# FFN matmuls that read their moving columns alternately from the two halves of a tile

## The chip, the cores and the metric

The kernel runs on one core of a Trainium2 chip. Its time is the device time of one execution in microseconds (us); the number compared is the median of several runs.

## The reference

The program computes a linear-attention layer with a decaying state (4 batches, 8 heads, 768 steps, 48 columns a head) and feeds its output to a two-layer network with a sigmoid GELU. The second part takes most of the time:

```python
def _moe_ref(x, w_in, w_out):        # x: 3072 x 384, w_in: 384 x 2048, w_out: 2048 x 384
    h = x @ w_in
    g = h * (1.0 / (1.0 + np.exp(-1.702 * h)))
    return (g @ w_out).astype(np.float32)
```

## The kernel before

Work is held transposed: features lie on the 128 partitions and tokens along the free dimension. The 3072 tokens are cut into 24 chunks of 128, and six groups of four chunks (512 tokens, `WIDE`) go through the FFN. Each group has 16 tasks, one for every 128 of the 2048 hidden features, 96 tasks in all.

The FFN is held to fp32 accuracy by splitting. Every operand is a pair of FP32R tensors, a rounded high part and the small rest, and each product is three matmuls: high by high, high by low, low by high. A task of the first product is 3 feature blocks by 3 terms, so 9 matmuls of 512 moving columns into one PSUM bank `ph`; a task of the second product is again 9, three for each of the banks `po0` to `po2`, which add up over the 16 tasks of a group. The moving operand of the first product is `xs[i][:, part, c, cs]`, a contiguous run of 512 4-byte words on each partition; that of the second is `gh` or `gl`, also 512 contiguous words.

Between the two products `gelu` runs: ScalarE writes `gh` (line 395) and `gf` (line 396) from the bank `ph`, and VectorE their difference `gl` (line 397).

The first 32 tasks, and the last one, use the whole 128-row array: `first_product` (lines 384 to 386) and `second_product` (lines 410 to 412). Tasks 32 to 94 are split into two halves of 64 rows (`first_rows`, `second_rows`, all through line 436 in `on_rows`). The two halves of the array run at the same time, one matmul of 64 rows in each; which of them stand side by side is written out in `rows_of`. A half of a matmul with 64 rows also has 512 columns.

The attention chunks (`chunk`) are put between the FFN tasks by an order written by hand: the string `RAMP` up to task 31, the list `PARTS` after it. It has its own small matmuls (lines 264 to 354), VectorE scans, and ScalarE work. `keep_clock` (line 425) are filler matmuls of 512 bf16 columns of zeros that stand in the first 46 us, before the FFN has data.

When a group is done, `store` copies each `po` bank to SBUF with one ScalarE instruction (line 511), 512 columns in order, and starts its DMA to the output. For the last group the third copy comes after the last matmul.

TensorE takes its instructions in the order of the program. Each matmul has its own load of 128 weight columns (PEld in the profile), which runs while the matmul ahead of it is streaming.

Of the kernel before, what the change touches and what calls it, by code (L numbers as in the profile page):

```python
# [13 lines left out]
AF = mybir.ActivationFunctionType  # L14
# [12 lines left out]
C = P  # L27
# [3 lines left out]
NF = DFF // P  # L31
NM = DM // P
# [8 lines left out]
W_SCALE = 2.0 ** 8  # L41
# [41 lines left out]
def rwkv_ffn_kernel(ctx: ExitStack, tc, wkr, vp, vrk, ub, w_in, w_out, masks, vt, uc, out):  # L83
    nc = tc.nc
    V, A, G, T = nc.vector, nc.scalar, nc.gpsimd, nc.tensor
# [27 lines left out]
        out=after, in_=after, pattern=[[1, C]], base=0, channel_multiplier=-1,  # L113
# [85 lines left out]
    def weight(which, f, m):  # L199

        s, n = divmod(f * NM + m, WP // P)
        return (pairs[2 * s + which][:, t, n * P : (n + 1) * P] for t in range(2))
# [172 lines left out]

    xs, po, parts, measures, tiled, steady = {}, {}, {}, {}, [], []

    def first_product(j, task):
        i, c0, c1, f = task
        cs = slice(c0 * C, c1 * C)  # L380
        ph = ps_h.tile([P, WIDE], F32, tag="ph", name="ph")[:, 0 : (c1 - c0) * C]
        for c in range(NM):
            h_, l_ = weight(0, f, c)
            T.matmul(ph, h_, xs[i][:, 0, c, cs], start=c == 0, stop=False)  # L384
            T.matmul(ph, h_, xs[i][:, 1, c, cs], start=False, stop=False)  # L385
            T.matmul(ph, l_, xs[i][:, 0, c, cs], start=False, stop=c == NM - 1)  # L386
        parts[j] = ph

    def gelu(j, task):
# [10 lines left out]
    def second_product(j, task):  # L400
        i, c0, c1, f = task
        gh, gl = parts.pop(j)
        first = i not in po
        if first:
            po[i] = [ps_o.tile([P, WIDE], F32, tag=f"po{m}", name=f"po{m}") for m in range(NM)]
        for m in range(NM):
            h_, l_ = weight(1, f, m)
            o = po[i][m][:, c0 * C : c1 * C]

            T.matmul(o, h_, gh, start=first, stop=False, skip_group_check=True)  # L410
            T.matmul(o, l_, gh, start=False, stop=False, skip_group_check=True)  # L411
            T.matmul(o, h_, gl, start=False, stop=f == NF - 1, skip_group_check=True)  # L412

    idle = []

# [17 lines left out]
    def on_rows(half, bank, out, w, x, start, stop, done):  # L433

        rows = slice(half * HB, (half + 1) * HB)
        mm = T.matmul(out, w[rows], x[rows], start=start, stop=stop, skip_group_check=True)  # L436
        before = relay.pop(bank, None)
        if before:
            tc.add_manual_dep(mm.ins, before, SYNC, reason="the bank's other row tile is done")
        if done:  # L440
            nop = nc.sync.nop()  # L441
            tc.add_manual_dep(nop.ins, mm.ins.name, SYNC, reason="a row tile is done with a bank")
            relay[bank] = nop.ins.name

    def first_rows(j, half):

        i, c0, c1, f = TASKS[j]
        cs = slice(c0 * C, c1 * C)
        if half == 0:
            parts[j] = ph_tile(c1 - c0)  # L450
        for n in range(3 * NM):
            c, term = divmod(n, 3)
            h_, l_ = weight(0, f, c)
            w, x = ((h_, 0), (h_, 1), (l_, 0))[term]
            end = n == 3 * NM - 1
            on_rows(
                half, ("h", j), parts[j], w, xs[i][:, x, c, cs],
                half == 0 and n == 0, half == 1 and end, half == 0 and end,
            )
            yield  # L460

    def second_rows(j, half):

        i, c0, c1, f = TASKS[j]
        gh, gl = parts[j]
        for n in range(3 * NM):
            m, term = divmod(n, 3)
            m = (m + half) % NM
            h_, l_ = weight(1, f, m)
            w, g = ((h_, gh), (l_, gh), (h_, gl))[term]  # L470
            tiles = po.setdefault(i, [None] * NM)
            start = tiles[m] is None
            if start:
                tiles[m] = ps_o.tile([P, WIDE], F32, tag=f"po{m}", name=f"po{m}")
            on_rows(
                half, ("o", i, m), tiles[m][:, c0 * C : c1 * C], w, g,
                start, f == NF - 1, term == 2,
            )
            yield
# [25 lines left out]
    def store(i, start, N, order=range(NM)):  # L505

        for m in order:
            o = po[i][m]
            ob = pools["late"].tile([P, WIDE], F32, tag="ob", name="ob", bufs=3)[:, 0:N]
            late = m != order[0] and isinstance(start, int) and start + N == NTOK  # L510
            A.activation(ob, o[:, 0:N], AF.Copy, scale=1.0 / W_SCALE)
            (A if late else queue[0]).dma_start(out[m, :, bass.ds(start, N)], ob)
        po.pop(i)
        xs.pop(i)
# [5 lines left out]
    with tc.manual_schedule():  # L520
# [17 lines left out]
        def do(token):  # L538
            kind, i = token[0], int(token[1:] or 0)
            told[token] = told.get(token, 0) + 1  # L540
            if kind in "lamwrf":
                piece(kind, i)
                if kind == "w" and all(told.get(f"w{n}") == 4 for n in range(2 * NL)):
                    early.close()
                    pools["late"] = fast.enter_context(tc.tile_pool(name="late", bufs=2))
            elif kind == "x":
                group, col = where[i]
                if col == CHUNKS[group] - 1:
                    fill_x(xs[group], 0, (col + 1) * C)
            elif kind == "u":  # L550
                nc.sync.dma_start(u_sb, ub)
            elif kind == "M":
                A.dma_start(hm[TOP:R2], masks)
                for x in states + [v[:, 0:TOP] for v in values]:
                    G.memset(x, 0.0)
            elif kind == "k":
                for _ in range(i):
                    keep_clock()
            elif kind == "g":
                first_product(i, TASKS[i])  # L560
            elif kind == "h":
                gelu(i, TASKS[i])
            elif kind == "y":
                second_product(i, TASKS[i])
            if kind == "y" or kind == "r" and told[token] == 2:
                i -= LAG if kind == "r" else 0
                parts.pop(i, None)
                group = TASKS[i][0]
                if i == last[group]:
                    store(group, starts[group] * C, CHUNKS[group] * C, (1, 0, 2) if kind == "r" else range(NM))  # L570
# [58 lines left out]
    with tc.If(n < full):  # L629
# [5 lines left out]
        with tc.tile_pool(name="gp", bufs=1) as gp, tc.tile_pool(name="ob", bufs=2) as ob, tc.For_i(0, B, 1) as b:  # L635
            pools["late"] = ob
            xg = [new_x(i) for i in range(2)]
            for p in range(NP):
# [7 lines left out]
                for d in range(D):  # L646
                    rows = []
                    for i, c0 in enumerate((1 + p * CW, 1 + NP * CW + p * C, 1 + NP * CW + NP * C + p * C)):
                        x = gp.tile([R2, CB, C], F32, tag=f"row{i}", name=f"row{i}", bufs=2)
# [16 lines left out]
                for half in range(2):  # L666
                    x = xg[half]
# [3 lines left out]
            for half in range(2):  # L671
                xs[half] = xg[half]
                for f in range(NF):
                    task = half, 0, 3, f
                    first_product(f, task)
                    gelu(f, task)
                    second_product(f, task)
                store(half, b * S + half * 384, 384)
# [54 lines left out]
```

## Time and profile before

| | us |
|---|---|
| median of 3 runs | 528.33 |
| the runs | 527.12, 528.33, 528.34 |
| span of the profiled execution, first to last instruction | 526.4 |
| TensorE matmul busy | 514.5 (98%) |
| TensorE weight loads busy | 437.0 (83%) |
| VectorE busy | 295.8 (56%) |
| ScalarE busy | 284.5 (54%) |

The profiled execution is known by its span; the median of the runs is 1.9 us longer, which is what lies ahead of the first and behind the last instruction. A matmul's record covers its way through the array, so records of matmuls that follow one another overlap: what one costs in a dense stretch is the step from start to start, not its duration.

### The profile page before, as it was taken

To read this page: it belongs to the slowest core of one execution; us is meant where nothing else is said; L and a number is where in the kernel's file an instruction comes from. 1 tells how busy PE (TensorE), PEld (TensorE's weight loads), DVE (VectorE), ACT (ScalarE), POOL (GpSimd) and SP (SyncE) were. 2 spreads that over 40 slices of the span, in tenths; PEclk is the share of its full clock that TensorE was granted. 3 is DMA by queue.
4 is the path that set the end of the run, shared out by engine and by line. 5 is a ranking of instruction groups with operands and counts; after the bars stand their busy time and mean duration, and the time that the engine had idled before them with its cause. 6 is when DMAs were issued, how large, how long until landed. Compare 5 with 4: busy or idle time off the path is not lost.

```text
span 526.4 us, 11132 instructions
## 1 busy us (share of the span) xinstructions
PE 514.5 (98%) x4539; PEld 437.0 (83%) x4539; DVE 295.8 (56%) x447; ACT 284.5 (54%) x609; POOL 42.6 (8%) x93
## 2 busy tenths in 40 slices
PE   7999999999999999999999999999999999999995
PEld 3766888888888888899999899999988998888873
DVE  7899999999884215656455455555555322111110
ACT  3988989877754714635445546545545422323222
POOL 2002000002000200201003021003020002100000
PEclk9999999999999999999999999999999999999999
DMA  8997921045633300152104062204050001100001
GB/s 291 289 393 215 346 93 61 2 164 140 220 110 107 76 0 1 45 183 86 67 2 136 2 226 61 91 2 137 2 159 1 1 1 31 61 2 1 0 1 66
DMA packets 14938, 50.95 MB, mean 97 GB/s; under 512 B 2336, under 2 KB 4384, under 8 KB 14880
## 3 DMA queue, kind: packets, MB, share of 16 engines
q1 hardware_dynamic: 9792, 31.83, 17.8%
q0 software_dynamic: 4688, 17.82, 11.0%
q8 instruction: 37, 0.61, 0.5%
q10 hardware_dynamic: 400, 0.53, 0.3%
q14 instruction: 21, 0.17, 0.1%
HBM read 43.09 MB, written 4.72 MB: 91 GB/s over the span
## 4 chain that ended last, share of the span: by engine, by line
PE 89%; DVE 2%; ACT 1%; DMA 1%; POOL 1%; issue 0%; ACTq 0%; SPq 0%
PE po L436 26%; PE ph L436 24%; PE ph L384 5%; PE po L410 4%; PE ph L385 4%; PE ph L386 4%; PE po L411 4%; PE po L412 4%; PE ps_y L346 4%; PE ps_s L331 4%; PE ps_y L354 3%; PE ps_u L312 1%; DMA x<-x 1%; POOL x L372 1%; DVE am L334 0%; PE ps_t L290 0%
## 5 line engine op out<-in xcount | busy, mean ns | idle before, releaser
L436 PE MATMUL ph<-x,pair 64*128 64x512 f32 x1134 | 194.1, 387 | 0.0
L397 DVE TENSOR_TENSOR gl<-gf,gh 128x512 fp32r<-128x512 f32 x96 | 66.3, 690 | 192.9 <-ACT gf L396 192.6
L436 PE MATMUL po<-gh,pair 64*128 64x512 f32 x768 | 165.6, 396 | 0.2 <-SPq L441 0.2
L436 PEld LDWEIGHTS ph<-x,pair 64*128 64x128 f32 x1134 | 148.8, 184 | 11.3
L395 ACT ACTIVATE gh<-ph 128x512 fp32r<-128x512 f32 x96 | 57.4, 598 | 175.7 <-PE ph L436 149.9
L436 PEld LDWEIGHTS po<-gh,pair 64*128 64x128 f32 x768 | 97.9, 185 | 10.6 <-issue 1.2
L436 PE MATMUL po<-gl,pair 64*128 64x512 f32 x384 | 104.0, 388 | 0.0
L301 ACT ACTIVATE am<-ident,s 128x128 f32<-128x128 f32 x192 | 58.8, 394 | 2.7 <-issue 1.6
L396 ACT ACTIVATE gf<-ph 128x512 f32<-128x512 f32 x96 | 57.1, 595 | 0.0
L436 PEld LDWEIGHTS po<-gl,pair 64*128 64x128 f32 x384 | 51.4, 184 | 4.9
L384 PE MATMUL ph<-x,pair 128*128 128x512 f32 x99 | 39.7, 401 | 0.5 <-DMA x<-x 0.5
L372 POOL DMA_DIRECT2D x<-x x36 | 18.2, 512 | 260.5 <-DVE x L206 260.5
L386 PE MATMUL ph<-x,pair 128*128 128x512 f32 x99 | 38.6, 390 | 0.0
L385 PE MATMUL ph<-x,pair 128*128 128x512 f32 x99 | 38.6, 390 | 0.0
L410 PE MATMUL po<-gh,pair 128*128 128x512 f32 x96 | 38.4, 400 | 0.0
L411 PE MATMUL po<-gh,pair 128*128 128x512 f32 x96 | 37.4, 390 | 0.0
L412 PE MATMUL po<-gl,pair 128*128 128x512 f32 x96 | 37.4, 390 | 0.0
L211 ACT ACTIVATE junk<-lp 112x1032 bf16<-112x1032 f32 x24 | 25.6, 1068 | 9.9 <-DVE lp L241 9.7
L235 DVE TENSOR_TENSOR_SCAN lp<-wkr_t,d1r 112x516 f32<-112x516 f32 x24 | 29.4, 1226 | 1.5 <-POOL after L112 1.2
L241 DVE TENSOR_TENSOR_SCAN lp<-wkr_t,d1f 112x516 f32<-112x516 f32 x24 | 29.5, 1228 | 0.4
L346 PEld LDWEIGHTS ps_y<-am,v_t 128*64 128x64 f32 (+1 forms) x384 | 21.0, 130 | 9.9 <-issue 5.0
L346 PE MATMUL ps_y<-am,v_t 128*64 128x128 f32 (+1 forms) x384 | 27.7, 279 | 0.7 <-DVE am L334 0.5
(79 smaller groups left out, 622.9 us busy)
## 6 DMA issues: line engine op xcount, KB each, us to landing
wkr_t<-in_wkr SPq DMA_DIRECT2D x13, 770.5 KB, 4.7
wkr_t<-in_wkr POOLq DMA_DIRECT2D x8, 770.5 KB, 4.9
raw<-in_w_out SPq DMA_DIRECT2D x6, 1024.0 KB, 10.4
raw<-in_w_in SPq DMA_DIRECT2D x5, 1024.0 KB, 10.7
rk_t<-in_vrk POOLq DMA_DIRECT2D x9, 384.0 KB, 4.8
out_t<-ob POOLq DMA_DIRECT2D x12, 256.0 KB, 2.7
v_t<-in_vrk SPq DMA_DIRECT2D x15, 192.0 KB, 4.5
rk_t<-in_vrk SPq DMA_DIRECT2D x7, 384.0 KB, 3.6
```

What stands on the lines that cost most here:

```text
L301: A.activation(x_[:, p], ident, AF.Copy, scale=s[:, 2 * p + h : 2 * p + h + 1])
L346: T.matmul(ps[head(h), p], v[:, c : c + HB - h * TOP], am[h][:, p], start=p == 0, stop=sf is None and p == NP - 1, skip_group_check=True,)
L384: T.matmul(ph, h_, xs[i][:, 0, c, cs], start=c == 0, stop=False)
L385: T.matmul(ph, h_, xs[i][:, 1, c, cs], start=False, stop=False)
L386: T.matmul(ph, l_, xs[i][:, 0, c, cs], start=False, stop=c == NM - 1)
L395: A.activation(gh, ph, AF.Gelu_apprx_sigmoid, scale=1.0 / W_SCALE)
L396: A.activation(gf, ph, AF.Gelu_apprx_sigmoid, scale=1.0 / W_SCALE)
L397: V.tensor_tensor(gl, gf, gh.bitcast(F32), op=ALU.subtract)
L410: T.matmul(o, h_, gh, start=first, stop=False, skip_group_check=True)
L411: T.matmul(o, l_, gh, start=False, stop=False, skip_group_check=True)
L412: T.matmul(o, h_, gl, start=False, stop=f == NF - 1, skip_group_check=True)
L436: mm = T.matmul(out, w[rows], x[rows], start=start, stop=stop, skip_group_check=True)
```

## The change

Each moving operand of the FFN is handed over as a three-dimensional pattern. Where the 512 words were read as 0, 1, 2, 3, ..., they are read as 0, 256, 1, 257, 2, 258, ...: the address goes up 1 KiB, comes back, and is one word (4 bytes) further. The output pattern is written as 256 pairs, but its addresses are contiguous as before. So the columns of `ph` stand in another order than the tokens, those of `gh` and `gl` do likewise, and the second product, which reads alternately again, shifts them once more. After both, token number 128 c + b stands in column 4 b + c of `po`. The copy out of PSUM (line 511 before) reads with a step of 4 words, 128 at a time, and writes `ob` in token order. The number of instructions, their sizes, weights, buffers and order stay as they are. The fillers of `keep_clock` and the matmuls of the attention are untouched. For the groups of 384 tokens in the fallback at the end (which these inputs don't enter) the halves are 192 words.

```diff
+    def halves(x):
+        return x.rearrange("p (a b) -> p b a", a=2)
+    def by_twos(x):
+        return x.rearrange("p (b a) -> p b a", a=2)
...
-            T.matmul(ph, h_, xs[i][:, 0, c, cs], start=c == 0, stop=False)
-            T.matmul(ph, h_, xs[i][:, 1, c, cs], start=False, stop=False)
-            T.matmul(ph, l_, xs[i][:, 0, c, cs], start=False, stop=c == NM - 1)
+            T.matmul(by_twos(ph), h_, halves(xs[i][:, 0, c, cs]), start=c == 0, stop=False)
+            T.matmul(by_twos(ph), h_, halves(xs[i][:, 1, c, cs]), start=False, stop=False)
+            T.matmul(by_twos(ph), l_, halves(xs[i][:, 0, c, cs]), start=False, stop=c == NM - 1)
...
-            o = po[i][m][:, c0 * C : c1 * C]
-            T.matmul(o, h_, gh, start=first, stop=False, skip_group_check=True)
-            T.matmul(o, l_, gh, start=False, stop=False, skip_group_check=True)
-            T.matmul(o, h_, gl, start=False, stop=f == NF - 1, skip_group_check=True)
+            o = by_twos(po[i][m][:, c0 * C : c1 * C])
+            T.matmul(o, h_, halves(gh), start=first, stop=False, skip_group_check=True)
+            T.matmul(o, l_, halves(gh), start=False, stop=False, skip_group_check=True)
+            T.matmul(o, h_, halves(gl), start=False, stop=f == NF - 1, skip_group_check=True)
...
-        mm = T.matmul(out, w[rows], x[rows], start=start, stop=stop, skip_group_check=True)
+        mm = T.matmul(by_twos(out), w[rows], halves(x[rows]), start=start, stop=stop, skip_group_check=True)
...
-            A.activation(ob, o[:, 0:N], AF.Copy, scale=1.0 / W_SCALE)
+            A.activation(
+                ob.rearrange("p (c b) -> p c b", c=4), o[:, 0:N].rearrange("p (b c) -> p c b", c=4),
+                AF.Copy, scale=1.0 / W_SCALE,
+            )
```

## Rows read from the trace of the kernel before

**Rows 1.** The page: busy time, granted clock in 40 slices, chain by engine.

```profile
PE 514.5 (98%) x4539; PEld 437.0 (83%) x4539; DVE 295.8 (56%) x447; ACT 284.5 (54%) x609; POOL 42.6 (8%) x93
...
PEclk9999999999999999999999999999999999999999
...
PE 89%; DVE 2%; ACT 1%; DMA 1%; POOL 1%; issue 0%; ACTq 0%; SPq 0%
```

**Rows 2.** Windows: busy time by engine (instructions), granted clock, DMA share, GB/s.

```profile
8.60:50.00 41.40, 39.82 (x405) 27.68 (x404) 38.35 (x61) 33.67 (x77) 3.15 (x6) 1.00 0.91 303
50.00:200.00 150.00, 150.00 (x1013) 124.04 (x1014) 113.16 (x158) 106.72 (x217) 5.96 (x12) 1.00 0.37 122
200.00:510.00 310.00, 309.17 (x3065) 275.89 (x3065) 136.82 (x218) 137.50 (x306) 30.43 (x57) 1.00 0.17 55
```

**Rows 3.** Groups of TensorE by shape, whole span: count, busy us, mean ns.

```profile
L436 PE MATMUL ph<-x,pair 64*128 64x512 f32 x1134 | 194.1, 387 | 0.0
L436 PE MATMUL po<-gh,pair 64*128 64x512 f32 x768 | 165.6, 396 | 0.2 <-SPq L441 0.2
L436 PE MATMUL po<-gl,pair 64*128 64x512 f32 x384 | 104.0, 388 | 0.0
L384 PE MATMUL ph<-x,pair 128*128 128x512 f32 x99 | 39.7, 401 | 0.5 <-DMA x<-x 0.5
...
L410 PE MATMUL po<-gh,pair 128*128 128x512 f32 x96 | 38.4, 400 | 0.0
```

**Rows 4.** Chain from 190 to 192.2 us: start, length, what.

```profile
189.91 0.23 PE ph L384
...
192.18 0.23 PE po L411
```

**Rows 5.** Groups of TensorE by shape, from 470 to 490 us.

```profile
L436 PE MATMUL ph<-x,pair 64*128 64x512 f32 x90 | 15.4, 386 | 0.0
L436 PE MATMUL po<-gh,pair 64*128 64x512 f32 x60 | 12.3, 386 | 0.0
...
L436 PE MATMUL po<-gl,pair 64*128 64x512 f32 x30 | 7.8, 386 | 0.0
```

**Rows 6.** Timeline from 190.1 us: weight loads between matmuls of the whole array.

```profile
190.20 0.19 PEld L384 LDWEIGHTS ph<-x,pair 128*128 128x128 f32 x1
...
190.43 0.19 PEld L385 LDWEIGHTS ph<-x,pair 128*128 128x128 f32 x1
...
190.66 0.19 PEld L386 LDWEIGHTS ph<-x,pair 128*128 128x128 f32 x1
```

**Rows 7.** Line 425, from 3.6 to 8.5 us: duration min/median/max, first and last start.

```profile
L425 PE MATMUL idle<-d1r x13: 583/631/632, 3.1 to 8.2; 112*128 112x512 bf16 x13
```

**Rows 8.** Line 425, from 41 to 43.2 us.

```profile
L425 PE MATMUL idle<-d1r x12: 379/379/380, 40.7 to 43.1; 112*128 112x512 bf16 x12
```

**Rows 9.** Groups of ScalarE by shape: 185, 186 read every second word.

```profile
L185 ACT ACTIVATE raw<-raw 128x1024 int32<-128x1024 uint32 x12 | 13.9, 1158 | 0.0
L186 ACT ACTIVATE c<-raw 128x1024 f32<-128x1024 f32 x12 | 13.8, 1151 | 1.0 <-DVE pair L196 1.0
L194 ACT CAST pair<-c 128x1024 fp32r<-128x1024 f32 x12 | 12.5, 1054 | 1.7 <-DVE c L191 1.5
```

**Rows 10.** Groups of VectorE by shape: 188 works on every second word.

```profile
L188 DVE SCALAR_TENSOR_TENSOR raw<-raw 128x1024 int32<-128x1024 int32 x12 | 14.6, 1218 | 0.0
L196 DVE TENSOR_TENSOR pair<-c,pair 128x1024 fp32r<-128x1024 f32 x12 | 14.5, 1216 | 0.3 <-ACT pair L194 0.3
```

**Rows 11.** Line 511, whole span: duration min/median/max, first and last start.

```profile
L511 ACT ACTIVATE ob<-po x18: 577/597/629, 136.8 to 520.5; 128x512 f32<-128x512 f32 x18
```

**Rows 12.** Timeline of TensorE from 300.2 us, at a change of groups.

```profile
300.34 1.75 PE L436 MATMUL ph<-x,pair 64*128 64x512 f32 x13
301.75 0.50 PE L436 MATMUL po<-gh,pair 64*128 64x512 f32 x1
```

**Rows 13.** Timeline of ScalarE from 300 us, at the same change of groups.

```profile
301.12 1.06 ACT L511 ACTIVATE ob<-po 128x512 f32<-128x512 f32 x2
```

**Rows 14.** Waits: engine, line, what for; us in total, times, longest.

```profile
DVE gl L397 <- ACT gf L396: 192.6, 77, 7.5
ACT gh L395 <- PE ph L436: 149.9, 61, 3.9
```

## The prediction

> **What bounds the kernel now.** I read the page first. TensorE's matmul row is busy for 98% of the span, and the chain that ended last runs over TensorE for 89% of it [rows 1]. Busy time alone would not decide, since records of matmuls overlap; the chain does, and so do the windows: from 50 to 510 us TensorE is never idle for more than a microsecond in sum, while VectorE and ScalarE are busy for 113 and 107 of the first 150 us and for less than half of the 310 us after them [rows 2]. The granted clock stands in the highest tenth in all slices and at 1.00 in these windows, the upper level of 2.4 GHz [rows 1, 2]. The waits agree from the other side: the long ones are of the engines behind TensorE, ScalarE for `ph` (149.9 us) and VectorE for ScalarE (192.6 us), and those cost nothing [rows 14].
>
> Next comes what TensorE spends. The groups by shape give 3 x 99 matmuls of the first product and 3 x 96 of the second on the whole array, 585 in all (lines 385, 386 and 411, 412 repeat the counts of 384 and 410), and 1134 + 768 + 384 = 2286 half-array matmuls, which run two at a time, so 1143 pairs [rows 3]. That is 1728 slots of 512 columns.
>
> The length of a slot is a step from start to start. On the whole array the chain takes ten of them from 189.91 to 192.18 us, so 0.227 us each [rows 4]. For pairs, 180 half-matmuls fall into a window of 20 us; since those that only overlap its edge count too, their starts cover 20.0 + 0.386 us, so 20.39 / 90 = 0.227 us a pair [rows 5]. 1728 x 0.227 = 392 us of the span of 526.4 is FFN streaming; 134 us are the attention's small matmuls, the fillers and the head and tail.
>
> What sets the 0.227 us? The weight loads start 0.23 us apart, in step with the matmuls, and one takes 0.19 us [rows 6], so they are close to being the limit themselves. The fillers, which have 512 columns too, stood 2.4 / 11 = 0.218 us apart between 40.7 and 43.1 us [rows 8]. So the columns alone need no more than 0.218 us, 2.35 columns a nanosecond, and about 0.01 us of each slot would hide a read that is slightly slower.
>
> **The change part by part.**
>
> *The moving reads* are all that matters. 1728 slots lie on the chain, with nothing beside them that could cover a longer one: they are what the other engines wait for. The trace of before has no matmul that reads in steps, so the price is bounded from both sides.
>
> From below: nothing. VectorE's instructions on every second word take 1218 ns, those on adjacent words 1216 ns [rows 10]; ScalarE's take 1158 and 1151 against 1054 ns, 9 to 10% more [rows 9]. Up to about 4% (0.218 to 0.227 us) the slot hides it, at 10% it would be 0.240 us and 1728 x 0.013 = 22 us.
>
> From above in the likeliest form: half the rate, one new address for every word where now adjacent words can come together. What 512 columns cost at half the rate is seen in this trace, whatever slowed them there: the first fillers stood 5.1 / 12 = 0.425 us apart, with records of 631 ns where later ones have 379 ns [rows 7, 8]. A slot would be 0.425 us if only the columns counted, or 0.227 + (0.425 - 0.218) = 0.434 us if today's slot were lengthened by the difference. That is 0.198 to 0.207 us more a slot, 342 to 358 us over 1728.
>
> I take the upper side, 0.430 us. The stepped rows that cost 0 to 10% are of engines which take 1024 words in 1216 or 1054 ns, 0.84 to 0.97 words a nanosecond, and in their patterns two used words still lie only 8 bytes apart. The moving operand takes 2.35 words a nanosecond, almost three times as many, and after the change no two consecutive words are nearer than 1020 bytes. A port that serves 2.35 adjacent words a nanosecond has to fetch more than a word at a time unless it fetches that often; the second word of each fetch is what alternate reading throws away, unless it is kept until it is asked for two words later. The row that this is nearest to is the half-rate filler, not the stepped copy.
>
> The Trainium skill speaks of this on its page "SBUF — State Buffer" (section Specifications (TRN2)): SBUF is read in lines of 16 bytes, and full bandwidth needs at least two hits on a line. By that rule each of the 512 words would be the only hit on its line in a row, and the rate would be about half, the sum above. No row of the kernel before shows it for matmuls.
>
> *The outputs of the matmuls* keep contiguous addresses: 0. A third dimension in the pattern adds no instruction: 0.
>
> *ScalarE and VectorE between the products* read and write contiguous columns as before; with longer slots they have more time, not less: 0.
>
> *The copy out of PSUM* reads in steps of four words. It takes 597 ns, 18 times [rows 11]. From below 0; from above it doubles, +0.6 us. The last copy of the last group is on the path to the end: 0 to 0.6 us. The others stand at the five changes of groups, where ScalarE's copies start at 301.12 us, while TensorE has 13 half-matmuls of the first product from 300.34 us on and goes on with `po` at 301.75 us [rows 12, 13]; that cover grows with the slots (if the change costs nothing there, a copy twice as long would put up to 0.6 us into each change, 3 us in all). I take the row that it is nearest to, the stepped ScalarE rows of +10%, so 0.1 us in all.
>
> *What could take something back:* attention work that now holds TensorE up. In the windows from 50 us on there is under 1 us of it in the busy row [rows 2]; short gaps between starts within overlapping records could hold some 10 us more. I count none and let the range have it. VectorE, 93% busy up to 50 us [rows 2], is ahead of the FFN and isn't touched.
>
> Sum: 526.4 + 1728 x 0.203 + 0.1 = 526.4 + 350.8 + 0.1 = 877.3 us of span, and with the 1.9 us by which the median stands above the profiled span, about **880 us**, +67%. With 0.425 and 0.434 us a slot it is 870 and 887; gaps taken back make it 860, and other small losses (stores, 1% of the slots) 905.
>
> **The rivals.**
>
> *Alternate reading is free* (the other side). If the port keeps what it fetched until the second word is asked for two reads later, two streams that each go forward one word at a time are served as fast as one. For it: each half is walked in order, so every fetched word is used in the end; there is 0.01 us of cover in each slot; VectorE's stepped rows cost nothing [rows 10]. Against it: ScalarE's rows do cost something [rows 9], at a third of the rate. It decides from the point where 512 columns arrive within 0.227 us. Time: 526.4 + 0.1 + 1.9 = 528.4 us, or up to 3 us more with the stores.
>
> The Trainium skill has a measurement that leans this way, on "Vector Engine (DVE) Microarchitecture Reference" (section 5.2, Measured stream behaviour on trn2): there a single read stream of VectorE that alternated between two regions 16 KiB apart ran at the full rate, though hopping at every word on one of two sources made an operation about 1.6 times as long. By the first sentence this rival would hold and the time stay at 528; no row here shows either for TensorE.
>
> *A part of the penalty.* Fetches overlap, so that a slot lies between 0.24 and 0.41 us. For it: the range between the ends is wide and only the ends have rows. At 0.35 us the time is 528 + 1728 x 0.123 = 741 us.
>
> *More than half is lost.* If single words came no faster than the other engines' ports take them, 0.84 a nanosecond [rows 10], 512 of them would take 0.61 us: 528 + 1728 x 0.383 = 1190 us. Against it: nothing shows that TensorE's port works at their pace.
>
> *The granted clock falls* to 1.2 GHz because the array waits for words. The FFN slots would stay near 0.43 us, and of the other 134 us most would double: about 990 us. Against it: TensorE issues without a pause, and the clock was 1.00 in all windows [rows 2].
>
> **How the numbers follow.** Half the rate 0.47; free 0.27; a part 0.13; more than half lost 0.08; clock 0.03; some gain from the other order of words, for which I see no mechanism, 0.02. Below 0.3% (1.6 us) two medians of this kernel can't be told apart from no change; faster 0.02, same 0.27, slower 0.71. The likeliest case alone lies in 860 to 905 us. A range that leaves out at most 2 in 10 must also hold the free case and the part: 526 to 905 us, which leaves out about 0.13.
>
> **What would show it.** In the profile after: starts of lines 384 to 386 in the chain 0.43 us apart and records near 0.6 us with the granted clock still at 1.00; pairs the same; fillers and attention matmuls unchanged; the chain on TensorE for over 90%; ScalarE's wait for `ph` about doubled. Steps of 0.227 us would prove the free rival, anything between the partial one. The line-511 copy near 0.6 us shows its step right, near 1.2 us the upper bound. The prediction fails if the moving port keeps fetched words, because the whole sum hangs on that one price.

## The result, and the profile after

The changed kernel takes 515.99 us (median of 4 runs, 515.07 to 516.61) against 528.07 us (4 runs). The ratio is 0.9774, with a 95% interval of 0.976 to 0.9788: 2.3% faster, where 880 us was forecast. The profiled execution of the changed kernel took 516.61 us with a span of 514.9 us, 11.5 us less than before.

The page after, with busy time, granted clock and the chain by engine (beside [rows 1]):

```profile
PE 496.3 (96%) x4539; PEld 420.8 (82%) x4539; DVE 301.2 (59%) x447; ACT 289.6 (56%) x609; POOL 42.7 (8%) x93
...
PEclk9999999999999999999999999999999999999998
...
PE 74%; DVE 10%; ACT 5%; issue 2%; DMA 2%; POOL 1%; ACTq 0%; DVEq 0%; SPq 0%
```

TensorE is still what the chain runs over, but for 74% in place of 89%; VectorE, which had 2%, now has 10%, and its busy time has grown by 5.4 us though it does the same work. The same windows as in [rows 2]:

```profile
50.00:200.00 150.00, 143.68 (x1001) 121.60 (x1002) 117.90 (x157) 110.66 (x214) 5.99 (x12) 1.00 0.37 122
200.00:510.00 310.00, 307.57 (x3124) 269.50 (x3122) 138.80 (x221) 142.43 (x315) 30.53 (x57) 1.00 0.18 57
```

From 50 to 200 us TensorE, which was never idle there before, is idle for 6.3 us. The steps of the whole array in the chain (first and last of the 12 pieces between 190 and 192.2 us, beside [rows 4]):

```profile
189.79 0.22 PE po L418
...
192.16 0.22 PE ph L394
```

Eleven steps in 2.37 us are 0.2155 us each; before it was 0.227. And the pairs in a dense stretch, groups of TensorE from 440 to 460 us (count, busy, mean ns; beside [rows 5]):

```profile
L444 PE MATMUL ph<-x,pair 64*128 64x512 f32 x98 | 15.6, 376 | 0.0
L444 PE MATMUL po<-gh,pair 64*128 64x512 f32 x60 | 12.0, 379 | 0.0
L444 PE MATMUL po<-gl,pair 64*128 64x512 f32 x30 | 7.6, 376 | 0.0
```

That is 188 halves in 20 + 0.376 us, or 0.217 us a pair against 0.227. A matmul record is 376 ns long in place of 386. So a slot is shorter when the words are read alternately: 1728 slots shorter by 0.0109 us (0.2267 to 0.2158, by the start times in the traces, on the whole array and in pairs) are 18.8 us. Only 11.5 us arrive at the end. Where the rest went is seen in the weight conversions (`convert`), VectorE's first and then ScalarE's (count, busy, mean ns; beside [rows 9, 10]):

```profile
L188 DVE SCALAR_TENSOR_TENSOR raw<-raw 128x1024 int32<-128x1024 int32 x12 | 18.2, 1517 | 0.0
L191 DVE SCALAR_TENSOR_TENSOR c<-c,raw 128x1024 int32<-128x1024 int32 x12 | 17.0, 1419 | 0.4
...
L196 DVE TENSOR_TENSOR pair<-c,pair 128x1024 fp32r<-128x1024 f32 x12 | 14.5, 1215 | 0.1
```

```profile
L186 ACT ACTIVATE c<-raw 128x1024 f32<-128x1024 f32 x12 | 16.8, 1402 | 0.8 <-DVE pair L196 0.8
L185 ACT ACTIVATE raw<-raw 128x1024 int32<-128x1024 uint32 x12 | 16.8, 1397 | 0.0
L194 ACT CAST pair<-c 128x1024 fp32r<-128x1024 f32 x12 | 12.4, 1042 | 3.0 <-DVE c L191 2.7 <-DVE s L267 0.4
```

Line 191 before:

```profile
L191 DVE SCALAR_TENSOR_TENSOR c<-c,raw 128x1024 int32<-128x1024 int32 x12 | 14.7, 1226 | 0.4
```

The four lines that read or write every second word have become longer, line 188 from 1218 to 1517 ns, line 191 from 1226 to 1419, line 185 from 1158 to 1397 and line 186 from 1151 to 1402; those on adjacent words (196, 194) have not. Here is one of the places where TensorE now stands still (timeline of TensorE from 86 us):

```profile
88.28 0.38 PE L420 MATMUL po<-gl,pair 128*128 128x512 f32 x1
90.34 0.48 PE L392 MATMUL ph<-x,pair 128*128 128x512 f32 x1 [1.68 <-ACT gf L404]
```

The next task's first product waits for a `ph` bank, which ScalarE has yet to read. Last, the first start of the pairs (their weight loads: min/median/max, first and last start), before and then after:

```profile
L436 PEld LDWEIGHTS ph<-x,pair x1134: 183/184/188, 209.1 to 510.6; 64*128 64x128 f32 x189
```

```profile
L444 PEld LDWEIGHTS ph<-x,pair x1134: 183/186/188, 211.3 to 499.4; 64*128 64x128 f32 x189
```

The first 32 tasks end 2.2 us later than before, with shorter slots; the pairs then make up 13.4 us. The copy out of PSUM with its step of four words costs nothing (line 519, beside [rows 11]):

```profile
L519 ACT ACTIVATE ob<-po x18: 584/596/622, 142.3 to 508.9; 128x512 f32<-128x512 f32 x18
```

### The profile page after: what moved, and what is told of

It reads as the page before. It is cut to its first block, busy times and chain, and to the rows that moved or that the text cites. A ratio compares the mean times of both kernels' runs of the same rounds, so it can differ in the third digit from the quotient of the medians.

```text
span 514.9 us, 11207 instructions
## 1 busy us (share of the span) xinstructions
PE 496.3 (96%) x4539; PEld 420.8 (82%) x4539; DVE 301.2 (59%) x447; ACT 289.6 (56%) x609; POOL 42.7 (8%) x93
## 4 chain that ended last, share of the span: by engine, by line
PE 74%; DVE 10%; ACT 5%; issue 2%; DMA 2%; POOL 1%; ACTq 0%; DVEq 0%; SPq 0%
PE po L444 25%; PE ph L444 24%; PE ps_y L346 3%; PE ps_s L331 3%; DVE raw L188 3%; PE po L418 3%; PE ps_y L354 3%; PE po L420 2%; PE po L419 2%; PE ph L392 2%; PE ph L393 2%; PE ph L394 2%; PE ps_u L312 1%; DVE pair L196 1%; DVE c L191 1%
## 5 line engine op out<-in xcount | busy, mean ns | idle before, releaser
L444 PE MATMUL ph<-x,pair 64*128 64x512 f32 x1134 | 185.4, 376 | 0.0
L444 PE MATMUL po<-gh,pair 64*128 64x512 f32 x768 | 157.7, 385 | 0.2 <-SPq L449 0.2
L444 PEld LDWEIGHTS ph<-x,pair 64*128 64x128 f32 x1134 | 143.5, 186 | 14.0
L444 PEld LDWEIGHTS po<-gh,pair 64*128 64x128 f32 x768 | 95.6, 186 | 10.6 <-issue 1.1
L444 PE MATMUL po<-gl,pair 64*128 64x512 f32 x384 | 99.2, 376 | 0.0
L444 PEld LDWEIGHTS po<-gl,pair 64*128 64x128 f32 x384 | 50.0, 186 | 4.8
L392 PE MATMUL ph<-x,pair 128*128 128x512 f32 x99 | 38.9, 393 | 3.5 <-ACT gf L404 2.9
L394 PE MATMUL ph<-x,pair 128*128 128x512 f32 x99 | 37.6, 380 | 0.1
L393 PE MATMUL ph<-x,pair 128*128 128x512 f32 x99 | 37.5, 379 | 0.0
L418 PE MATMUL po<-gh,pair 128*128 128x512 f32 x96 | 37.3, 389 | 0.1
L419 PE MATMUL po<-gh,pair 128*128 128x512 f32 x96 | 36.4, 380 | 0.0
L235 DVE TENSOR_TENSOR_SCAN lp<-wkr_t,d1r 112x516 f32<-112x516 f32 x24 | 29.4, 1224 | 1.4 <-DMA wkr_t<-in_wkr 1.1
```

The source lines that it names most:

```text
L392: T.matmul(by_twos(ph), h_, halves(xs[i][:, 0, c, cs]), start=c == 0, stop=False)
L393: T.matmul(by_twos(ph), h_, halves(xs[i][:, 1, c, cs]), start=False, stop=False)
L394: T.matmul(by_twos(ph), l_, halves(xs[i][:, 0, c, cs]), start=False, stop=c == NM - 1)
L418: T.matmul(o, h_, halves(gh), start=first, stop=False, skip_group_check=True)
L419: T.matmul(o, l_, halves(gh), start=False, stop=False, skip_group_check=True)
L444: mm = T.matmul(by_twos(out), w[rows], halves(x[rows]), start=start, stop=stop, skip_group_check=True)
```

## The experiments

Three questions were open: what makes the slot shorter, what the half rate of the prediction belongs to, and what takes 7 us back.

**The form of the pattern or the order of the words.** The patterns stay three-dimensional, the words are read in order:

```diff
     def halves(x):
-        return x.rearrange("p (a b) -> p b a", a=2)
+        return x.rearrange("p (b a) -> p b a", a=2)
```

> Same three-dimensional patterns as the changed kernel, 256 pairs, but the moving words are read at contiguous addresses and the copy out of PSUM is the old one. Theory A (the order of the addresses shortens the slot): slots back at 0.227 us, time 528 us, no change. Rival B (the form of the pattern, pairs instead of one run of 512, shortens the slot): slots at 0.216 us, time 516 us.

Measured: 527.47 us, ratio 0.9995 (0.9983 to 1.0007). Two steps from the chain of this kernel near 190 us:

```profile
191.86 0.23 PE po L418
192.09 0.23 PE po L419
```

Theory A holds: the order of the addresses does it.

**Where the time is given back.** Alternate reading in some token groups only (`i >= 2`, and `i < 2` in the second kernel); the others read in order and have the old copy. Against the changed kernel, shortened:

```diff
+    def alternate(i):
+        return i >= 2
...
-    def halves(x):
-        return x.rearrange("p (a b) -> p b a", a=2)
+    def halves(x, i):
+        return x.rearrange("p (a b) -> p b a" if alternate(i) else "p (b a) -> p b a", a=2)
```

> Alternate reading only in the token groups 2 to 5 (tasks 32 to 95: 1143 pairs of half-array matmuls and 9 whole ones, 1152 slots); groups 0 and 1 read contiguously. Theory R (what the first 32 tasks gain is lost there again, since TensorE then waits for ScalarE and VectorE): 1152 x 0.011 = 12.6 us are gained and nothing is given back, time 515 to 516.5 us, as fast as the whole change. Rival (the gain is given back in equal parts everywhere): 12.1 x 1152 / 1728 = 8.1 us, time 520 us.

> Alternate reading only in the token groups 0 and 1 (tasks 0 to 31 on the whole array, 576 slots). Theory R: 576 x 0.011 = 6.3 us are gained in the slots and about as much is lost in new waits between 50 and 130 us, time 526.5 to 528.5 us. Rival (equal parts): 12.1 x 576 / 1728 = 4 us, time 524 us.

Measured: groups 2 to 5 alone 514.39 us, ratio 0.9746 (0.9725 to 0.9768), and groups 0 and 1 alone 529.88 us, ratio 1.0042 (1.0024 to 1.006). The first is a little under the 515 to 516.5 us of theory R. The gain comes from the groups 2 to 5 alone; in the first two the same reading makes the kernel a little slower, more than the 526.5 to 528.5 us that theory R allowed, which hadn't the longer conversions in it. VectorE's line 188 in the second kernel:

```profile
L188 DVE SCALAR_TENSOR_TENSOR raw<-raw 128x1024 int32<-128x1024 int32 x12 | 18.2, 1517 | 0.0
```

and in the first:

```profile
L188 DVE SCALAR_TENSOR_TENSOR raw<-raw 128x1024 int32<-128x1024 int32 x12 | 14.6, 1218 | 0.0
```

**The price of a pattern by itself.** A kernel with bursts of one line each:

```python
for i in range(48): T.matmul(out, W[:, i % 2], X[:, 0:512], ...)                                        # contiguous
for i in range(48): T.matmul(out, W[:, i % 2], X[:, 0:512].rearrange("p (a b) -> p b a", a=2), ...)     # halves
```

> No FFN and no attention: bursts of 48 FP32R matmuls of 512 moving columns, back to back, each burst with another read pattern of the moving operand; only the starts from burst line to burst line are read. Contiguous: 0.227 us a slot by both theories. Theory A: the same addresses as 256 pairs 0.227, alternate halves 0.216, alternate at other distances (258, 260, 264, 512, 1024 words) shows whether the distance matters; steps of 2, 3, 4 words and quarters and eighths show whether any read that doesn't take adjacent words in a row is as quick, or is slower as the prediction had it (0.43). Rival B: every pattern of more than one dimension 0.216. Rival C (the slot is set by the weight loads): with 64 weight columns instead of 128 the contiguous slot falls to 0.216 as well; by A it stays at 0.227. bf16 contiguous: 0.216 to 0.218 as the fillers.

> Bursts of 48 matmuls as in the first table of patterns, without anything else. Theory P (even and odd columns are fetched as two streams, each by itself, and what counts is the step s from a column to the next but one: s of 1 word gives 0.216 us, 2 words 0.227, 4 words and more 0.45): halves with every second word 0.227, halves with every fourth word 0.45, two adjacent words of every four 0.45, two of eight 0.45, four of eight 0.227, each word twice 0.216, pairs swapped 0.227, backwards 0.227; bf16 halves 0.216, bf16 every second 0.216 to 0.227, bf16 every fourth (8 bytes) 0.45. Rival Q (adjacent words fetched together are what is quick, and two interleaved runs are an exception): halves with every second word 0.45, two of four at most 0.235, each word twice 0.227.

Some of the first kernel's matmuls by line (duration min/median/max, first and last start, so that the difference over 47 is the slot): in order (108), in order as pairs (109), halves (110), quarters (124), every second word (126), in order with 64 weight columns (137).

```profile
L108 PE MATMUL o<-X,W x48: 389/389/389, 27.7 to 38.3; 128*128 128x512 f32 x48
...
L109 PE MATMUL o<-X,W x48: 389/389/389, 38.5 to 49.2; 128*128 128x512 f32 x48
...
L110 PE MATMUL o<-X,W x48: 378/379/379, 49.4 to 59.6; 128*128 128x512 f32 x48
...
L124 PE MATMUL o<-X,W x48: 434/448/454, 204.3 to 217.6; 128*128 128x512 f32 x48
...
L126 PE MATMUL o<-X,W x48: 629/629/631, 241.3 to 262.5; 128*128 128x512 f32 x48
...
L137 PE MATMUL o<-X,W x48: 387/392/442, 394.5 to 405.3; 128*64 128x512 f32 x48
```

And of the second: halves with every second word (109), halves with every fourth (110), two adjacent words of every four (112), each word twice (115), bf16 halves (122).

```profile
L109 PE MATMUL o<-X,W x48: 387/389/399, 38.9 to 49.6; 128*128 128x512 f32 x48
...
L110 PE MATMUL o<-X,W x48: 615/630/637, 49.8 to 71.1; 128*128 128x512 f32 x48
...
L112 PE MATMUL o<-X,W x48: 622/629/631, 87.9 to 109.1; 128*128 128x512 f32 x48
...
L115 PE MATMUL o<-X,W x48: 379/379/379, 142.8 to 152.9; 128*128 128x512 f32 x48
...
L122 PE MATMUL o<-Z x48: 644/646/647, 216.8 to 239.6; 128*128 128x512 bf16 x48
```

The slots of both kernels, as means over 47 starts:

| order of the 512 words read | us a slot |
|---|---|
| halves; alternately 4, 8, 16, 128, 257, 260, 264, 512 or 1024 words apart; each word twice | 0.216 |
| halves, starting at an odd word; 258 apart | 0.217 |
| one word for all columns | 0.219 |
| in order; in order as pairs; pairs swapped; halves with every second word; alternately 2 words apart | 0.227 to 0.228 |
| in order, starting at word 1 or 2; backwards; four of eight | 0.233 to 0.237 |
| alternate runs of 16 or 4 words | 0.240, 0.250 |
| quarters, one word of each in turn | 0.283 |
| alternate runs of 2 words; two of three | 0.340 |
| every second, third or fourth word; two of four or of eight; halves with every fourth word | 0.450 to 0.460 |
| eighths, one word of each in turn | 0.488 |
| bf16: in order, every second, every fourth, halves | 0.216, 0.226, 0.451, 0.484 |

Rival C falls: with half the weight columns the slot in order is 0.231 us, no shorter, and the halves have 0.216. So does rival Q. Theory P orders most of the table: what counts for FP32R is how far a column is from the next but one. At a distance of one word (halves, alternately 4 words apart and more, each word twice) a slot is 0.216, of two (in order) 0.227, of three (two of three) 0.340, of four or more mostly 0.45, whether the other column is next to it or 4 KiB away. It missed on bf16 halves, where it expected 0.216, and three FP32R rows don't fit: quarters have 0.283 and alternate runs of 2 words 0.340, though the next column but one is over 100 words away in both, and one word for all columns has 0.219. Nor does it say why the start of a run matters (0.233 to 0.237). Two streams, one for the even columns and one for the odd ones, are what the rows look like; they don't show how the port is built.

**Beside the other engines.** The first attempt put VectorE and ScalarE beside the bursts, and they ran ahead of TensorE, so its phases didn't coincide:

> No FFN and no attention: eight phases, in each a burst of 76 FP32R matmuls of one read pattern on TensorE, and beside it on VectorE and ScalarE five instructions on every second word (1024 words, the form of the weight conversion) and then five on adjacent words. Theory C (alternate reading takes more of the memory's turns, and instructions that read or write every second word lose them): every second word on VectorE 1.22 us beside nothing and beside contiguous reading, about 1.5 us beside the alternate halves; ScalarE's 1.15 and 1.4 us; on adjacent words 1.22 and 1.05 us in all phases. Rival D (the longer conversions in the changed kernel have another cause, such as the weight DMAs that land at that time): no difference between the phases. For alternation within 8 words (distance of 4 words) theory C has no number: near 1.22 us if the distance matters, near 1.5 us if only the order does.

Read by the time of day, VectorE's instructions on every second word had 1.66 to 1.83 us while TensorE read halves, and 1.22 us while it alternated at 4 words. Theory C had a point, though it had put the first number at 1.5, and the distance seemed to matter. The phases were run again in step:

> The table of phases once more with the engines held in step (each phase begins on all three when the phase before has ended, and with 24 contiguous matmuls ahead of the pattern), and with more distances: the two runs that are read alternately lie 4, 8, 16, 64, 128, 256, 258, 260, 264, 288 or 1024 words apart. No FFN and no attention. Theory C1 (contention grows with the distance: the two words of a pair in neighbouring lines disturb nobody): every second word on VectorE 1.22 us beside 4 words apart, about 1.7 us from some distance on. Theory C2 (certain distances collide, powers of two for instance): 1.7 us beside 128, 256 and 1024 apart, 1.22 us beside 4, 260, 264 and 288. Rival (every alternate reading disturbs alike): 1.7 us beside all of them.

Groups in four of its phases, from the stretch with every second word; first TensorE reading in order:

```profile
L140 DVE SCALAR_TENSOR_TENSOR d<-d 128x1024 int32<-128x1024 int32 x4 | 4.9, 1224 | 0.1
L141 ACT ACTIVATE e<-e 128x1024 f32<-128x1024 f32 x4 | 4.8, 1204 | 0.1
```

halves, 256 words apart:

```profile
L155 ACT ACTIVATE e<-e 128x1024 f32<-128x1024 f32 x4 | 7.2, 1800 | 0.1
L154 DVE SCALAR_TENSOR_TENSOR d<-d 128x1024 int32<-128x1024 int32 x4 | 7.0, 1760 | 0.1
```

4 words apart:

```profile
L168 DVE SCALAR_TENSOR_TENSOR d<-d 128x1024 int32<-128x1024 int32 x4 | 4.9, 1224 | 0.1
L169 ACT ACTIVATE e<-e 128x1024 f32<-128x1024 f32 x4 | 4.7, 1174 | 0.1
```

260 words apart:

```profile
L253 ACT ACTIVATE e<-e 128x1024 f32<-128x1024 f32 x4 | 4.9, 1227 | 0.1
L252 DVE SCALAR_TENSOR_TENSOR d<-d 128x1024 int32<-128x1024 int32 x4 | 4.9, 1226 | 0.1
```

VectorE has 1.76 or 1.77 us beside 64, 128, 256 and 1024 words apart, 1.69 beside 258, and 1.22 to 1.23 beside 4, 8, 16, 260, 264 and 288, and beside TensorE's own every second word. ScalarE goes with it (1.76 to 1.81, 1.72, and 1.17 to 1.23). On adjacent words both keep 1.22 to 1.24 and 1.05 to 1.08 in every phase. TensorE's slot is 0.216 at all these distances of alternate reading (0.217 at 258), so it doesn't pay. Of the three theories C2 holds: certain distances disturb. All that do are multiples of 64 words (256 bytes) but for 258; they are powers of two as well, and no multiple such as 192 was run, so which of the two it is stays open.

**In the kernel.** Alternation in the groups 1 to 5, while group 0, in whose time the weights are converted, reads in order (`i >= 1` above); and then everywhere, but at another distance:

```diff
     def halves(x):
-        return x.rearrange("p (a b) -> p b a", a=2)
+        return x.rearrange("p (g a c) -> p g c a", a=2, c=4)     # c=64 and c=32 in two others
```

> Alternate reading in the token groups 1 to 5; group 0 (tasks 0 to 15, 48 to 135 us, in which the weights are converted) reads contiguously. Theory C: the conversions keep 1.22 and 1.15 us and the 288 slots of group 1 gain 288 x 0.011 = 3.1 us more than with the groups 2 to 5 alone: 511 to 512 us. Rival R (VectorE alone bounds the time up to 150 us, whatever TensorE reads): the gain of group 1 is lost in waits, 514.4 us.

> The whole change, but alternating within blocks of 8 words (words 0, 4, 1, 5, 2, 6, 3, 7) in place of the two halves of the tile; the copy out of PSUM puts the order right in the same way. Slots 0.216 us as with the halves by the first table of patterns. If the distance decides over theory C's contention: conversions at 1.22 us and 509 to 512 us; if only the order of reading does: conversions at 1.4 to 1.5 us and 516 us, as the change.

> The whole change with the alternation inside blocks of 128 words, the two runs 64 words (256 bytes) apart. Slots 0.216 us. If what the phases showed holds in the kernel (distances that are a multiple of 64 words disturb instructions on every second word): conversions on VectorE 1.4 to 1.5 us, waits in the first 32 tasks as in the change, 516 us. If another property of the halves made the change wait: 510.7 us.

> The same with blocks of 64 words, the two runs 32 words (128 bytes) apart, which isn't a multiple of 64 words. If the rule of the distance holds: conversions 1.22 us, 510.7 us, as with 4 words. If the disturbance grows with the distance, something between 511 and 516 us.

| alternation | us | ratio (95%) | line 188, ns |
|---|---|---|---|
| groups 1 to 5, halves | 510.74 | 0.9682 (0.9657 to 0.9707) | 1217 |
| all, 4 words apart | 510.66 | 0.9676 (0.966 to 0.9692) | 1216 |
| all, 64 words apart | 515.77 | 0.9772 (0.9753 to 0.9791) | 1508 |
| all, 32 words apart | 510.27 | 0.9658 (0.9632 to 0.9685) | 1224 |

VectorE's line 188 at 64 and then at 32 words:

```profile
L188 DVE SCALAR_TENSOR_TENSOR raw<-raw 128x1024 int32<-128x1024 int32 x12 | 18.1, 1508 | 0.0
```

```profile
L188 DVE SCALAR_TENSOR_TENSOR raw<-raw 128x1024 int32<-128x1024 int32 x12 | 14.7, 1224 | 2.9 <-ACT c L186 2.9
```

The 2.9 us of idle time at 32 words go back to a DMA of weights, for which ScalarE's line 185 waited 3.2 us in that execution; the lengths of the conversions are not in question there.

The kernel does what the phases said: at 64 words it is the changed kernel again, at 4 and 32 it is 5 us faster than that, and these kernels differ in nothing but the distance and the order in the copy out of PSUM that goes with it. So 32 words, a power of two too, don't disturb. Alternate reading in group 0 gives nothing even where it disturbs nobody (510.66 us with it, 510.74 without), and in group 1 it gives 3.6 us (514.39 to 510.74). These three at 510 us beat both kernels.

**The forecast price.** Last, the order that should cost what the prediction said:

```diff
     def halves(x):
-        return x.rearrange("p (a b) -> p b a", a=2)
+        return x.rearrange("p (b a) -> p a b", a=2)     # even words, then odd words
```

> The whole change with another order: every FFN matmul reads the even words of its tile first and then the odd ones (a step of 2 words), and the copy out of PSUM puts the order right. By the tables of patterns a slot takes 0.451 us: 528 + 1728 x (0.451 - 0.227) = 915 us, more where VectorE and ScalarE are held up. This is the price that the prediction gave to alternate reading; if the tables don't carry over to the kernel, the time is nearer to 516 or 528 us.

Measured: 916.26 us, ratio 1.7338 (1.7288 to 1.7389). Two pieces of its chain, seven steps apart:

```profile
190.24 0.45 PE po L419
...
193.40 0.48 PE po L420
```

## Why the prediction was wrong

**What bounds the kernel** was right: 1728 slots on TensorE's chain, at 0.227 us, and a change of the slot goes to the end one for one where TensorE is the bound. With 0.451 us a slot the sum gives 915 us, and 916 were measured.

**The step that failed** is the price of the moving reads: "I take the upper side, 0.430 us", because "the second word of each fetch is what alternate reading throws away, unless it is kept until it is asked for two words later". The slot measured 0.216 us, 0.011 less than before where 0.203 more was summed. Two interleaved runs are served at least as fast as one, which fits the condition at the end of that sentence, though no run shows what the port keeps. The half rate exists, but for other orders: every second word (0.451 us), two of every four, halves with every fourth word. The rows chosen answered another question: the filler at half rate shows what a half rate costs, not which order has it. No row of before had the answer, and the free rival should have stood higher.

**That it could gain** was missed one step earlier. Weight loads that start 0.23 us apart and take 0.19 were read as "close to being the limit themselves". They only follow the matmuls: with 64 weight columns the slot in order stays at 0.231, and with all 128 the halves have 0.216. The filler's 0.218 us showed what 512 columns need, and the 0.01 us between the two was taken as cover for a slower read. It was the price of reading FP32R words in order, and it was there to be won: 18.8 us over all slots. In the sum it stood as nothing, and among the rivals a gain had a chance of 0.02 and no mechanism.

**"ScalarE and VectorE ... : 0"** failed too. Between the products they are as before, but the conversions beside them became longer: lines 188 and 191 by 12 x (0.299 + 0.193) = 5.9 us of VectorE. It was busy for 48.8 of the 50 us from 50 to 100 us before, the third busy time in this row (windows, as in [rows 2]):

```profile
50.00:100.00 50.00, 50.00 (x301) 41.48 (x302) 48.83 (x58) 46.74 (x84) 0.00 (x0) 1.00 0.43 150
```

In that stretch VectorE has no time to spare, so shorter slots give nothing (group 0: 288 slots, 3.1 us) and longer conversions are lost in full. 18.8 - 3.1 - 5.9 = 9.8 us should be left; 11.5 were measured in span. The first 32 tasks should end 5.9 us later for the conversions and 3.1 us earlier for the slots of group 1, so 2.8 us later, and did so by 2.2; the 1152 slots behind them should give 12.6 us, and 13.4 were measured. These last differences have no explanation. The runs bear out the two terms by themselves: group 0 gives nothing, and the kernels at 4 and 32 words, without the longer conversions, are 5.3 and 5.7 us faster than the changed one. What isn't separated is VectorE from ScalarE, whose lines 185 and 186 grew by 5.9 us too and which was busy for 46.7 of the same 50 us; for VectorE speaks its part of the chain, 2 to 10% where ScalarE's went from 1 to 5%. The prediction looked at VectorE's 93% up to 50 us and called it "ahead of the FFN"; its 113 of 150 us from 50 on is a mean that hid the stretch of 98%.

On the two pages of the Trainium skill: "SBUF — State Buffer", section Specifications (TRN2), asks for two hits on a line of 16 bytes; two adjacent words of every four have them and take 0.451 us, so for TensorE the runs don't bear it out. The same page of the Trainium skill, section Who interferes with whom, says that TensorE and ScalarE never wait on anyone; that ScalarE's instructions go from 1204 to 1800 ns beside alternate reading is against it. The single stream between two regions on the Trainium skill's page "Vector Engine (DVE) Microarchitecture Reference", section 5.2, that runs at full rate was the right hint for FP32R on TensorE (0.216 us), and not for bf16 (0.484 us).

**The rest:** the copy out of PSUM cost nothing (596 ns, forecast 0 to 10% more), the output side and the third dimension nothing (527.47 us with both), the clock stayed at 1.00 up to 510 us, and fillers and attention matmuls didn't change. In the prediction's sums the upper time for half the rate should read 886, not 887.

**Open:** why reading in order costs 0.011 us a slot and what makes quarters 0.283 us; the two streams are argued from a table of times, with exceptions in it. Why 64, 128, 256 and 1024 words disturb is open too, and so is what becomes of multiples of 64 that are no powers of two.

## What to carry to other kernels

A stride isn't slow or fast by its size: what a pattern costs was found in one kernel of bursts that prices some thirty patterns at once, and where the trace has no row for a step on which everything hangs, no argument from other engines' rows should narrow the range. A dense slot of FP32R matmuls at 0.227 us has 5% in it when two runs of words are read alternately; beside strided work of other engines the distance of the runs has to be tried (here 4 and 32 words disturbed nothing, 64 and 256 did). And a gain on the busiest engine is paid out only in the stretches where it is the bound: look for short stretches in which another engine is at 98%.

## What the runs showed of the hardware that was not expected

- Contiguous FP32R reading isn't the fastest order: 0.2267 us for 512 columns against 0.2158 for two interleaved runs, with records of 389 and 379 ns.
- A step of two 4-byte words halves TensorE's rate (0.451 us); a pair of adjacent words, then a hop, doesn't save it (0.340 to 0.460). For bf16 a step of two elements costs little (0.226 us), and the interleaved halves more than halve the rate (0.484).
- TensorE's order of reading makes VectorE's and ScalarE's instructions on every second word up to 1.5 times as long (1.22 to 1.77, 1.20 to 1.81 us), at distances of 64, 128, 256, 258 and 1024 words and not at 4, 8, 16, 260, 264 and 288; instructions on adjacent words and TensorE itself don't feel it.
